# Layer 1's second product in 7 products of half blocks, its scale and bias on the result, ScalarE exponents, a new order

## The chip, the cores and the metric

The kernel runs on 1 core of a Trainium2 chip. The metric is the device time of that core in microseconds. Before the change the median of 3 runs is 805.74 us (804.72 to 806.02). One execution was profiled; its span, from the first instruction to the last, is 802.9 us.

## The reference

Attention runs within chunks of 64 positions, and its result goes through two layers. Inputs and results are float32, except that the weights of the layers lie in memory as 64-bit words, which the kernel itself turns into float32.

```python
# q, k, v: 4 batches x 8 heads x 576 positions x 64
scores = q_c @ k_c.T / sqrt(64)                # within each chunk of 64
attn = exp(scores - max); attn /= sum + 1e-9
x = attn @ v_c                                 # as 2304 tokens x 512
h = x @ w_in                                   # layer 1: 512 x 2048
x = (s * relu(h)**2 + b) @ w_out               #          2048 x 512; s, b: one number each
h = x @ w2_in                                  # layer 2
out = (max(h, 0) + log1p(exp(-abs(h)))) @ w2_out
```

## The kernel before

**Products.** A float32 product is made of three products of rounded halves: `split` cuts an operand into a high part (a CAST on ScalarE, L955) and the rest (a subtraction on VectorE, L964), and TensorE multiplies high by high, high by low and low by high. So a block of 128 rows, 128 sums and N = 384 tokens takes three matmuls of 384 columns.

**First products.** Both layers' first products use a scheme that makes a 2 x 2 product of half blocks with 7 products in place of 8. `quad(ph, i, j, ...)` makes, in layer `ph`, four blocks of hidden rows of pair `i` (of 8) for the group `j` (of 3) of 768 tokens (two halves of 384): products 1 to 7 (L1375, six matmuls each), copies between accumulators (L1397), four sums (`sub`, L942), and four hidden blocks (`hidden`, L1407: Relu in layer 1, Softplus in layer 2). The operands of the scheme are sums of halves of x (`even_forms`, `odd_forms`, `forms`) and of the weights (`weights1`).

**Second products.** In layer 1, each hidden block is stored to memory (`hid`, 192 KB). Then six blocks of results (3 groups x 2 halves, `block`) each run over 16 hidden rows x 4 output blocks x 3 matmuls (L1554). Hidden rows are loaded back four at a time (768 KB), squared on ScalarE (L1523), scaled by s with b added (L807 or L809) and split. The output weights are converted in advance by `weights2`, stored in `spill` (512 KB a pair) and loaded and split during the first block. In layer 2 the second product is `second_by_blocks`: 7 products x 3 groups x 8 steps x 6 matmuls (L1710). For it `quad` forms four sums more of the hidden blocks and stores seven arrays (`kept`, `summed`), `weights2` forms four sums more of the weights and stores seven arrays (`forms2`), and the results of the products are added into four result blocks.

**Weights.** `convert` turns 512 words of each of 128 rows into float32: the exponent is cut out (VectorE, L850), moved (ScalarE Relu, L867), the mantissa is put together (VectorE, L880 and L894), the sign is merged into the exponent (VectorE, L908), and mantissa and exponent are multiplied (VectorE, L922).

**Order.** All DMAs are issued from SyncE (`load`, L817). The order of every engine's instructions is made by `Work.order`: it steps through a modelled time, and among the operations that can start next takes the one with the smallest key. The keys are due times, from formulas in the code or from the table `PLAN`. The model gives each step a cost, and takes 300 KB per us for DMA (`BYTES`) and 2.0 us for a load (`LOAD`). Where an operation may run on either of two engines, the same search decides. `warmed` puts matmuls without a result (L1877) where TensorE would otherwise stand idle. Attention's steps (scores L1189, transposes L1290, values L1309) are woven with the first quads of layer 1.

## Time and profile before

| | |
|---|---|
| median of 3 runs | 805.74 us (804.72 to 806.02) |
| span of the profiled execution | 802.9 us |
| TensorE busy | 787.6 us, 98% |
| VectorE busy | 635.3 us, 79% |
| ScalarE busy | 514.2 us, 64% |
| DMA | 180.27 MB, mean 225 GB/s |

No other time of the profiled execution is recorded. The span falls into stages: the start to 8.0 us, attention with the first quads of layer 1 to 85.5, a transition to 95.2, the rest of layer 1's first product to 247.4, its second product to 447.7, layer 2's first product to 624.6, its second product to 799.4, and the last stores. The edges are where the kind of matmul changes. A row of windows gives the busy time of each engine in such a stretch; PE is TensorE's matmuls, PEld its weight loads, DVE VectorE, ACT ScalarE, POOL GpSimd, SP SyncE. Lines such as L942 are lines of the kernel before.

### The profile page before, as it was taken

Reading aid. Unit: us, or ns where it says so; the run is one execution under the profiler, and the core shown is the slowest. Engines: PE = TensorE matmul, PEld = TensorE weight load, DVE = VectorE, ACT = ScalarE, POOL = GpSimd, SP = SyncE. Lnnn points to the kernel's source line nnn. Section 1 sums busy time; section 2 is a strip of 40 time slices with the busy share of each in tenths; the row PEclk is TensorE's granted clock in tenths of the full one; section 3 lists DMA queues with packets and bytes.
Section 4 is the critical chain, followed back from the end, with each engine's and each line's share of the span. In section 5 each row is a group of like instructions: output and inputs, shape, how many; then the busy total and the mean of one; then the engine's idle time right before and its main releaser. Section 6 shows DMA issues by size and latency. Waiting matters only on the chain.

```text
span 802.9 us, 14597 instructions
## 1 busy us (share of the span) xinstructions
PE 787.6 (98%) x5148; PEld 772.8 (96%) x5148; DVE 635.3 (79%) x1167; ACT 514.2 (64%) x1127; POOL 138.9 (17%) x161
## 2 busy tenths in 40 slices
PE   7999999999999999999999999999999999999998
PEld 5788999999999999999999999999999999999998
DVE  6999898998858998889946786888876777777765
ACT  5877766666659867676765765655655566555543
POOL 3644311111110222123302220112010000000000
PEclk9999999999999999999999999999999999999999
DMA  7863477787679576766630056775788977678851
GB/s 275 277 192 111 162 251 234 265 274 259 221 237 370 207 243 196 269 212 211 225 113 1 31 194 226 243 252 200 256 287 288 388 284 241 231 236 289 275 191 59
DMA packets 78041, 180.27 MB, mean 225 GB/s; under 512 B 8720, under 2 KB 52752, under 8 KB 77072
## 3 DMA queue, kind: packets, MB, share of 16 engines
q1 hardware_dynamic: 77968, 179.34, 66.1%
q8 instruction: 40, 0.66, 0.3%
q14 instruction: 33, 0.27, 0.1%
HBM read 111.15 MB, written 68.16 MB: 223 GB/s over the span
## 4 chain that ended last, share of the span: by engine, by line
PE 92%; DVE 5%; issue 1%; DMA 1%; ACT 1%; POOL 1%; SPq 0%; DVEq 0%; POOLq 0%; ACTq 0%
PE at L1375 19%; PE S L1375 13%; PE S L1554 9%; PE at L1554 9%; PE A L1375 9%; PE S L1710 8%; PE at L1710 8%; PE A L1554 6%; PE A L1710 5%; DVE operands L964 1%; PE at L1309 1%; PE at L1189 1%; DMA last<-spill 1%; PE at L1290 1%; DVE mx L1203 1%
## 5 line engine op out<-in xcount | busy, mean ns | idle before, releaser
L942 POOL TENSOR_TENSOR mem<-mem 128x256 f32<-128x256 f32 x120 | 105.0, 885 | 382.3 <-DVE mem L922 296.5
L964 DVE TENSOR_TENSOR operands<-mem,operands 128x384 fp32r<-128x384 f32 (+4 forms) x186 | 128.4, 709 | 38.6 <-ACT operands L955 37.2
L955 ACT CAST operands<-mem 128x384 fp32r<-128x384 f32 (+4 forms) x186 | 112.0, 622 | 58.6 <-PE at L1710 36.2
L964 DVE TENSOR_TENSOR operands<-last,operands 128x384 fp32r<-128x384 f32 (+2 forms) x184 | 108.3, 609 | 48.8 <-ACT operands L955 38.7
L955 ACT CAST operands<-last 128x384 fp32r<-128x384 f32 (+2 forms) x184 | 93.3, 528 | 58.1 <-PE at L1710 18.4
L1375 PE MATMUL at<-operands 128*128 128x384 f32 x624 | 121.0, 336 | 0.0
L1375 PEld LDWEIGHTS at<-operands 128*128 128x128 f32 x624 | 109.4, 188 | 0.5 <-DVE mem L942 0.2
L1710 PE MATMUL at<-operands 128*128 128x384 f32 x384 | 87.1, 334 | 0.0
L1710 PE MATMUL S<-operands 128*128 128x384 f32 x384 | 87.1, 334 | 0.0
L1554 PE MATMUL S<-operands 128*128 128x384 f32 x432 | 85.1, 335 | 1.0 <-ACT operands L955 0.8
L1554 PE MATMUL at<-operands 128*128 128x384 f32 x432 | 83.2, 334 | 0.0
L1375 PE MATMUL S<-operands 128*128 128x384 f32 x420 | 82.9, 336 | 0.0
L1554 PEld LDWEIGHTS S<-operands 128*128 128x128 f32 x432 | 75.7, 188 | 1.5 <-ACT operands L955 1.1
L1554 PEld LDWEIGHTS at<-operands 128*128 128x128 f32 x432 | 75.7, 188 | 0.0
L942 DVE TENSOR_TENSOR mem<-mem 128x384 f32<-128x384 f32 (+1 forms) x108 | 60.4, 566 | 19.2 <-ACT mem L1407 14.6
L1375 PEld LDWEIGHTS S<-operands 128*128 128x128 f32 x420 | 73.8, 188 | 0.1
L1710 PEld LDWEIGHTS at<-operands 128*128 128x128 f32 x384 | 68.4, 188 | 0.0
L1710 PEld LDWEIGHTS S<-operands 128*128 128x128 f32 x384 | 68.4, 188 | 0.0
L1375 PE MATMUL at<-last,operands 128*128 128x384 f32 x336 | 66.0, 336 | 0.6 <-ACT S L1397 0.6
L1407 ACT ACTIVATE mem<-S 128x384 f32<-128x384 f32 x104 | 50.4, 490 | 24.4 <-PE S L1375 21.8
L1375 PE MATMUL A<-operands 128*128 128x384 f32 x300 | 60.6, 340 | 1.3 <-DVE A L942 1.3
L1397 ACT COPY S<-at 128x384 f32<-128x384 f32 x80 | 37.3, 467 | 37.4 <-PE at L1375 33.0
(87 smaller groups left out, 1237.0 us busy)
## 6 DMA issues: line engine op xcount, KB each, us to landing
mem<-in_w_dram SPq DMA_DIRECT2D x64, 512.0 KB, 4.5
summed<-mem SPq DMA_DIRECT2D x168, 192.0 KB, 2.2
mem<-summed SPq DMA_DIRECT2D x30, 768.0 KB, 5.5
hid<-mem SPq DMA_DIRECT2D x96, 192.0 KB, 3.2
last<-hid SPq DMA_DIRECT2D x24, 768.0 KB, 5.4
last<-in_qk_dram SPq DMA_DIRECT2D x36, 256.0 KB, 3.7
last<-summed SPq DMA_DIRECT2D x12, 768.0 KB, 5.2
mem<-forms SPq DMA_DIRECT2D x7, 1024.0 KB, 7.0
```

The source lines that it names most:

```text
L942: lambda e: on(e).tensor_tensor(out=out(), in0=x(), in1=y(), op=op or ALU.subtract),
L955: lambda e: nc.scalar.copy(out=hi().bitcast(F32R), in_=x()),
L964: lambda e: nc.vector.tensor_tensor(out=lo().bitcast(F32R), in0=x(), in1=hi(), op=ALU.subtract),
L1189: nc.tensor.matmul(out_[c * D : (c + 1) * D, pr], of("q")[:, pr * P + c * D : pr * P + (c + 1) * D], kb[:, :, pr, c, :], start=True, stop= ...
L1203: lambda e: nc.vector.tensor_reduce(out=mx[:, :, 0], in_=heads(at(sc)), op=ALU.max, axis=AX.X),
L1290: nc.tensor.transpose(at(pt)[:, c], of("e")[:, c], ident)
L1309: nc.tensor.matmul(at(px)[y, x], of("v")[y, x], of("aT")[y, x], start=True, stop=True)
L1375: nc.tensor.matmul(acc(dst)().rearrange("p (u c) -> p u c", u=GROUP), l[a], r[c], start=start and kk == 0 and x == 0, stop=kk == 1 and x == 2,
L1397: lambda e: nc.scalar.copy(out=acc(place)(), in_=acc(ba)()),
L1407: lambda e: nc.scalar.activation(out=at(go), in_=acc(place)(), func=AF.Softplus if ph else AF.Relu),
L1554: nc.tensor.matmul(at(accs[d])[:, :N], l[a], r[c], start=m == 0 and z == 0, stop=m == NM - 1 and z == 2,)
L1710: nc.tensor.matmul(at(accs[d])[:, :N], l[a], r[c], start=i == 0 and y == 0, stop=i == NF - 1 and y == 2,)
```

## The change

Layer 1's second product becomes `second_by_blocks(0, ...)`, as in layer 2; `block`, `hid` and `spill` go. Therefore in layer 1, too, `quad` squares the four hidden blocks (on ScalarE or VectorE), forms the four further sums and stores seven arrays, and `weights2` forms and stores seven arrays of the weights. A pair of hidden blocks is now split in one step of 768 columns, in both layers.

The scale s and the bias b are applied to the result: b times the column sums of the weights. Those sums come from products with two more columns of ones (`edge`), so that in three of the 21 steps (products 1, 2 and 5 of the first group) the matmuls have 386 columns. The results are multiplied by s, with the bias added, on VectorE or ScalarE.

`convert` has two forms. In the one used for 44 of the 64 conversions (`leaky`) ScalarE makes the exponent from the words' upper 16 bits (or VectorE by a shift), and two Prelu steps on ScalarE give the exponent with the sign, so that the merge on VectorE goes. The other form is the former one.

Sums (`sub`) and the subtraction of a split may run on GpSimd or VectorE, as the table says. `PLAN` now holds a rank for each operation, with a letter where there is a choice of engine, and `Work.order` takes each engine's operations by rank. The last two pairs of layer 1's first product are now run group by group. Four of layer 2's eight pairs of `weights2`, and two of its `weights1`, come during layer 1's second product. 

```diff
-    BYTES = 300e3
+    STORE, LOAD, FIRST = 1.6, 2.3, 3.0
+    BYTES = 330e3
...
-    "quad0 4 1": (160.36, 93.12, 157.98, 159.24, 161.1, 163.91, 162.43, 143.76, 108.75, 166.77, 167.6, 162.14, 163.4, 164.01, 166.3, 167.57, 168.17, 170.46, 172.15, 173.14,),
...
+    "quad0 4 1": "908 913 923 932 938 947 965 970 983 979 982 930 942 956 951 961 966 1010 1028 1036V 1006 986 969 1040 1047G 1054 1058 1060 1075 1057 1078",
...
+        def exponent(e):
+            if e == "ACT":
+                halves = at(f).bitcast(I16).rearrange("p (a b) -> p a b", b=4)
+                nc.scalar.activation(
+                    out=a().bitcast(I32), in_=halves[:, :, 3], func=AF.Copy, scale=1 / 16, bias=-15 / 32
+                )
...
+        if leaky:
+            o1 = add(
+                {"ACT": act(DM), "DVE": dve(DM, True)}, key, exponent, [ld], [f, am], after=turn.get(("am", part), ())
+            )
...
+            o2 = add({"ACT": act(DM)}, key, leak(1.0, -896.0, 2.0**-40, af, ai), [o1], [am])
+            o5 = add({"ACT": act(DM)}, key, leak(2.0**23, 1792 * 2.0**-17, 2.0**40, ai, af), [o2], [am])
...
-    def sub(key, out, x, y, n, deps, uses=(), op=None, e="DVE", port=True, **kw):
+    def sub(key, out, x, y, n, deps, uses=(), op=None, port=True, **kw):
         return add(
-            {e: pool(n) if e == "POOL" else dve(n, port=port)},
+            {"DVE": dve(n)} | ({"POOL": pool(n)} if n < 512 else {}) if port else {"DVE": dve(n, port=False)},
...
-            out_ = lambda: hid[ph][2 * j + half][:, 2 * i + row]
-            st = load(key + 0.1, out_, lambda: at(go), P * N * 4, [o], [go])
-            hid_in.setdefault((ph, j, half), []).append(st)
-            quads_done[ph].append(st)
+
+            def square(e):
+                if e == "ACT":
+                    nc.scalar.activation(out=at(go), in_=at(go), func=AF.Square)
+                else:
+                    nc.vector.tensor_tensor(out=at(go), in0=at(go), in1=at(go), op=ALU.mult)
+
+            return go, add({"ACT": act(N), "DVE": dve(N)}, key, square, [o], [go])
...
-        if not ph:
-            return
...
+            edged = not ph and j == groups[0] and n in (1, 2, 5)
+            width = N + 2 if edged else N
...
+                if i % 2 == 0:
+                    pair = divided((a + i % 4 * N, 2 * N), key, ld)
+                hi, lo = [(x, width) for x, y in pair[i % 2]]
...
+                        add(
+                            {"ACT": act(N, False, 2), "DVE": dve(N, True, 2)},
+                            t,
+                            lambda e, dst=dst, x=to // 2 * 2 + d: scaled(e, mem(*dst, v), x),
+                            [biased[(5 if to > 1 else 2), d], *scalars],
+                            w=[dst],
+                        )
...
-    for z, x in enumerate(BLOCKS):
-        block(0, x // 2, x % 2, end + z * dt, z == 0)
+    second_by_blocks(0, end)
```

How the order moves, at three places. In these rows a name before the arrow is written, a name behind it read; `A_`, `S_` and `at_` are TensorE's accumulators, `operands` holds split operands, `mem` and `last` are working memory, and x6 counts equal instructions in a row. Lines of the new kernel are other lines than those of the one before.

TensorE at the end of attention, before: the last values step is L1309, products of layer 1 are L1375.

```order
L1375 MATMUL A_66<-operands 128x384 x6
L1375 MATMUL S_67<-operands 128x384 x6
L1375 MATMUL A_66<-operands 128x384 x6
L1290 MATMUL at_70<-ident,last_117 128x128 x4
L1309 MATMUL at_72<-last_117 64x64 x16
L1309 MATMUL at_70<-last_117 64x64 x16
L1375 MATMUL A_66<-operands 128x384 x6
L1375 MATMUL S_68<-operands 128x384 x6
L1375 MATMUL S_69<-operands 128x384 x6
L1290 MATMUL at_71<-ident,last_117 128x128 x4
L1375 MATMUL A_65<-operands 128x384 x6
L1309 MATMUL at_72<-last_117 64x64 x16
```

The same place after; values are L1421 there, transposes L1402, products L1487.

```order
L1421 MATMUL at_71<-last_134 64x64 x16
L1421 MATMUL at_72<-last_134 64x64 x16
L1402 MATMUL at_70<-ident,last_134 128x128 x4
L1421 MATMUL at_72<-last_134 64x64 x16
L1402 MATMUL at_70<-ident,last_134 128x128 x4
L1402 MATMUL at_71<-ident,last_134 128x128 x4
L1421 MATMUL at_70<-last_134 64x64 x16
L1421 MATMUL at_71<-last_134 64x64 x16
L1487 MATMUL A_66<-operands 128x384 x12
L1487 MATMUL A_65<-operands 128x384 x6
L1487 MATMUL A_66<-operands 128x384 x6
L1487 MATMUL S_67<-operands 128x384 x6
```

Before, single products stand between the last attention steps; after, the last eight steps of attention stand together and the products follow them. Ahead of the last values step stood 15 products, and now 7.

TensorE where layer 1's second product begins, before (first product L1375, second L1554).

```order
L1375 MATMUL A_66<-operands 128x384 x6
L1375 MATMUL at_72<-operands 128x384 x6
L1375 MATMUL S_68<-operands 128x384 x6
L1375 MATMUL A_65<-operands 128x384 x6
L1554 MATMUL S_67<-operands 128x384 x6
L1554 MATMUL at_71<-operands 128x384 x6
```

The same place after (first product L1487, second L1755).

```order
L1487 MATMUL S_69<-operands 128x384 x6
L1487 MATMUL at_72<-operands 128x384 x6
L1755 MATMUL S_69<-operands 128x386 x3
L1755 MATMUL at_70<-operands 128x386 x3
L1487 MATMUL S_67<-operands 128x384 x6
L1755 MATMUL S_69<-operands 128x386 x3
L1755 MATMUL at_70<-operands 128x386 x3
L1487 MATMUL A_65<-operands 128x384 x6
L1487 MATMUL S_68<-operands 128x384 x6
L1755 MATMUL S_68<-operands 128x384 x3
L1755 MATMUL at_71<-operands 128x384 x3
```

Before, the second product begins after the last product of the first; after, four half steps of it, with 386 columns, stand ahead of the last three products. On SyncE's queue at that place, before (`hid` and `spill` are the stores, `last` is where the second product's operands are loaded):

```order
L817 DMA hid_5_90<-mem 128x384
L817 DMA last_2578<-spill_91 128x512 x3
L817 DMA hid_5_90<-mem 128x384
L817 DMA last_2578<-hid_4_89 128x1536 x2
L817 DMA hid_0_85<-mem 128x384
L817 DMA last_2578<-spill_91 128x512 x6
L817 DMA hid_2_87<-mem 128x384
L817 DMA last_2578<-hid_4_89 128x1536
```

And after (`summed` and `forms` are stores where they are written, loads where they are read):

```order
L905 DMA last_2842<-summed_1_2_87 128x1536
L905 DMA summed_3_1_92<-mem 128x384
L905 DMA summed_7_2_105<-mem 128x384
L905 DMA last_2842<-forms_0_127 128x1024
L905 DMA summed_5_1_98<-mem 128x384
L905 DMA summed_4_2_96<-mem 128x384
L905 DMA summed_5_2_99<-mem 128x384
L905 DMA summed_2_1_89<-mem 128x384
L905 DMA last_2842<-summed_1_0_85 128x1536
L905 DMA summed_2_2_90<-mem 128x384
L905 DMA summed_6_2_102<-mem 128x384
L905 DMA last_2842<-summed_1_2_87 128x1536
```

Before, 9 stores of hidden blocks stand behind the first load of the second product; after, 27 stores of sums do, and the loads of sums and of weight forms are woven with them.

VectorE in the middle of layer 1's first product, before (L850 exponent, L880 and L894 mantissa, L908 sign, L922 product, L942 sum).

```order
L850 TENSOR_SCALAR mem<-mem 128x512
L880 TENSOR_SCALAR mem<-mem 128x512
L894 SCALAR_TENSOR_TENSOR mem<-mem 128x512
L908 SCALAR_TENSOR_TENSOR mem<-mem 128x512
L922 SCALAR_TENSOR_TENSOR mem<-mem 128x512
L942 TENSOR_TENSOR A_65<-at_70,mem 128x384
L850 TENSOR_SCALAR mem<-mem 128x512
L880 TENSOR_SCALAR mem<-mem 128x512
L894 SCALAR_TENSOR_TENSOR mem<-mem 128x512
L908 SCALAR_TENSOR_TENSOR mem<-mem 128x512
```

The same stage after (L947 exponent, L1016 and L1030 mantissa, L1044 product, L1064 sum, L1534 square).

```order
L1064 TENSOR_TENSOR mem<-at_72,mem 128x384
L1534 TENSOR_TENSOR mem<-mem 128x384
L1016 TENSOR_SCALAR mem<-mem 128x512
L1064 TENSOR_TENSOR mem<-mem 128x384
L1064 TENSOR_TENSOR mem<-mem 128x256
L1064 TENSOR_TENSOR mem<-mem 128x384
L1030 SCALAR_TENSOR_TENSOR mem<-mem 128x512
L1064 TENSOR_TENSOR mem<-at_71,mem 128x384
L1044 SCALAR_TENSOR_TENSOR mem<-mem 128x512
L1064 TENSOR_TENSOR mem<-mem 128x384
L947 TENSOR_SCALAR mem<-mem 128x512
L1064 TENSOR_TENSOR mem<-mem 128x256 x2
```

Before, a conversion has five rows on VectorE with few sums between them; after, it has three or four, and sums of 384 and 256 elements and a square stand between them.

## Rows read from the trace of the kernel before

**Rows 1.** Busy time of each engine, share of the span, and instructions (the page):
```profile
PE 787.6 (98%) x5148; PEld 772.8 (96%) x5148; DVE 635.3 (79%) x1167; ACT 514.2 (64%) x1127; POOL 138.9 (17%) x161
```

**Rows 2.** Windows: length, busy (instructions) by engine, granted clock, DMA share, GB/s:
```profile
8.00:85.50 77.50, 71.92 (x1048) 60.74 (x1044) 70.32 (x150) 61.08 (x214) 35.38 (x38) 1.00 0.65 215
...
95.20:247.40 152.20, 150.88 (x864) 149.48 (x862) 128.48 (x221) 96.78 (x193) 24.18 (x30) 1.00 0.76 252
...
247.40:447.70 200.30, 200.09 (x1152) 199.83 (x1153) 161.66 (x296) 143.60 (x294) 42.99 (x46) 1.00 0.59 193
...
447.70:624.60 176.90, 175.59 (x1011) 175.08 (x1010) 138.43 (x245) 106.02 (x218) 29.54 (x32) 1.00 0.66 229
...
624.60:799.40 174.80, 174.80 (x1009) 174.56 (x1008) 124.40 (x237) 96.91 (x192) 0.00 (x0) 1.00 0.72 245
```

**Rows 3.** Groups by line, TensorE, 0 to 85 us: busy, mean ns | idle before:
```profile
L1877 PE MATMUL S<-nought 128*128 128x512 f32 x31 | 10.3, 439 | 0.0
```

**Rows 4.** Groups kept apart by form, VectorE and ScalarE:
```profile
L908 DVE SCALAR_TENSOR_TENSOR mem<-mem 128x512 uint32<-128x512 uint32 x34 | 23.5, 692 | 1.2 <-ACT mem L867 1.2
...
L850 DVE TENSOR_SCALAR mem<-mem 128x512 uint32<-128x512 uint32 x34 | 15.7, 463 | 11.9 <-DMA mem<-in_w_dram 11.6
...
L964 DVE TENSOR_TENSOR operands<-mem,operands 128x1024 fp32r<-128x1024 f32 x15 | 18.8, 1256 | 0.0
...
L964 DVE TENSOR_TENSOR operands<-mem,operands 128x768 fp32r<-128x768 f32 x9 | 10.2, 1133 | 2.4 <-ACT operands L955 2.4
...
L802 DVE COPY last<-at 128x512 f32<-128x512 f32 x7 | 4.7, 674 | 0.5 <-ACT mem L1407 0.3 <-PE at L1290 0.2
...
L942 DVE TENSOR_TENSOR mem<-mem 128x256 f32<-128x256 f32 x6 | 2.5, 413 | 3.2 <-ACT mem L800 3.2
...
L867 ACT ACTIVATE mem<-mem 128x512 int32<-128x512 int32 x34 | 21.6, 635 | 17.9 <-DVE mem L850 17.9
...
L1523 ACT ACTIVATE last<-last 128x384 f32<-128x384 f32 x96 | 45.2, 515 | 5.9 <-DMA last<-hid 5.8
```

**Rows 5.** Timeline of VectorE, then ScalarE: start us, us, engine, line, operation:
```profile
540.69 0.69 DVE L908 SCALAR_TENSOR_TENSOR mem<-mem 128x512 uint32<-128x512 uint32 x1
541.29 0.55 DVE L942 TENSOR_TENSOR mem<-mem 128x384 f32<-128x384 f32 x1
541.76 0.69 DVE L922 SCALAR_TENSOR_TENSOR mem<-mem 128x512 f32<-128x512 f32 x1
...
455.95 0.49 ACT L1407 ACTIVATE mem<-S 128x384 f32<-128x384 f32 x1
456.34 0.61 ACT L955 CAST operands<-last 128x512 fp32r<-128x512 f32 x1
456.85 0.49 ACT L1407 ACTIVATE mem<-S 128x384 f32<-128x384 f32 x1
```

**Rows 6.** DMA, 95.2 to 247.4: total; issues with KB, us to landing:
```profile
DMA packets 18379, 38.38 MB, mean 252 GB/s; under 512 B 2288, under 2 KB 12427, under 8 KB 18367
...
hid<-mem SPq DMA_DIRECT2D x81, 192.0 KB, 3.3
...
spill<-mem SPq DMA_DIRECT2D x8, 512.0 KB, 5.3
```

**Rows 7.** Windows, as in rows 2, of three stretches with much DMA:
```profile
600.00:650.00 50.00, 50.00 (x290) 50.00 (x289) 33.75 (x64) 29.49 (x62) 0.00 (x0) 1.00 0.92 329
...
235.00:240.00 5.00, 5.00 (x30) 5.00 (x30) 2.29 (x4) 2.40 (x5) 0.00 (x0) 1.00 0.96 303
...
165.00:170.00 5.00, 5.00 (x30) 5.00 (x29) 4.45 (x9) 2.39 (x6) 1.84 (x3) 1.00 0.79 209
```

**Rows 8.** Windows as in rows 2: start of layer 2, and inside layer 1:
```profile
455.00:460.00 5.00, 3.69 (x21) 3.37 (x21) 3.56 (x7) 4.31 (x9) 1.43 (x2) 1.00 0.24 88
...
275.00:300.00 25.00, 25.00 (x146) 25.00 (x145) 23.85 (x44) 19.17 (x39) 4.51 (x5) 1.00 0.61 201
```

691 lines of the change are left out of this document (328 added, 363 removed), and 906 rows, old and new, of the table PLAN.

## Prediction

> **What bounds the kernel now.** I read the busy table first, then the stages, then the stages' other engines. The busy table gives TensorE 98% of the span [rows 1]. A busy share alone could hide slow matmuls, so the windows by stage come next; the granted clock is 1.00 in each, the level of 2.4 GHz [rows 2]. Layer 1's second product fills 247.40 to 447.70 with 1152 matmuls and layer 2's fills 624.60 to 799.40 with 1008 (the row counts one that straddles its edge); PE is busy for 200.09 of 200.30 us and all of 174.80. Both run at 0.174 us per matmul of 384 columns, back to back. The same holds in the two first products after 85.5 us. Only the attention stretch, 8.0 to 85.5, is otherwise: PE shows 71.92 busy, but 31 of its matmuls are fillers without a result [rows 3], and DVE is busy for 70.32 of 77.5 us. There DVE sets the pace; after it PE does. So a matmul taken from a back-to-back stage is worth its 0.174 us, provided that what feeds and empties PE still keeps up. That proviso is the question here, since the change buys its matmuls with DVE, ACT and DMA work in layer 1's first product.
>
> **The change part by part.** Durations are of one execution with a span of 802.9 us. The page records no other time of it; against the median of 805.74 shown, 2.84 us lie outside the span, and I add them back at the end.
>
> *Fewer matmuls.* 6 blocks of 16 x 12 (1152) become 7 products x 3 groups x 8 x 6 (1008). The kernel already holds both forms, so the price is a difference of two stages: 200.30 - 174.80 = 25.5 us [rows 2]. Three of the 21 steps run 386 columns instead of 384: 144 matmuls x 2/384 x 0.174 = 0.13 us. Term: **-25.4**.
>
> *Attention stretch.* The exponents go to ACT and the order is new. Up to the last reciprocal of the attention the new DVE order has four sign merges fewer (0.692 each), three exponent shifts (0.463), one split of 1024 (1.256) and one of 768 (1.133), four copies of 512 (0.674) and one difference of 384 (0.55), and two more sums of 256 (0.41): 2.77 + 1.39 + 1.26 + 1.13 + 2.70 + 0.55 - 0.83 = 9.0 us less on the engine that sets the pace [rows 4, 5]. But the last attention matmul now follows 7 products where it followed 15, by the order, and those 8 x 6 x 0.174 = 8.3 us are run afterwards: 0.7 us gained. The order drops 9 of the 31 fillers at 10.3/31 = 0.33 us each [rows 3], which says up to 3.0 us gained. Against it, ACT was busy for 61.08 of 77.5 us and takes at least 8 more conversions (0.635) and the four copies: about 69 us in a stretch of 68.5, so it could cost as much as it gives, up to +3. I take **-1.0**, next to the DVE sum.
>
> *Layer 1's first product, DVE and ACT.* Stretch 95.2 to 247.4, DVE busy 128.48 of 152.2, ACT 96.78 [rows 2]. Each of the 24 quads gains four sums and four squares of 384. By the new order 76 of the 96 sums and 19 of the squares stand on DVE, 77 squares on ACT, the other 20 sums on POOL. DVE also gains about 25 sums of 256 for the weights' forms; it loses some 30 sign merges and 18 exponent shifts, and ACT gains 48 conversions. By durations that is 128.5 + 95 x 0.55 + 25 x 0.41 - 30 x 0.69 - 18 x 0.46 = 162 us for DVE, and 96.8 + 77 x 0.515 + 48 x 0.635 = 167 us for ACT [rows 4]: both over 152. Durations overstate it, though. When the next instruction waits ready, it starts before the last one's row ends: a sum of 384 shows 0.55 but the next starts 0.47 later, an operation of 512 shows 0.69 and 0.60, on ACT 0.61 and 0.51, 0.49 and 0.38 [rows 5]. Packed, DVE's 221 rows cost 0.08 each less, 111 us, and the change adds 95 x 0.47 + 25 x 0.34 - 30 x 0.60 - 18 x 0.38 = 28 (0.34 and 0.38 are estimates, the 0.41 and 0.46 less 0.08): 139 of 152. ACT: 97 - 193 x 0.10 + 77 x 0.41 + 48 x 0.53 = 135. So 91% and 89%, with PE still last. The ends are 0 and +15 (167 - 152). I take **0**: the rows of a full engine are the nearest. What hides the squares and sums is PE; if the cover goes, PE waits for free accumulators.
>
> The Trainium skill, "VectorE: DVE Perf Modes", section "The DRAIN you can't avoid", says that the next Vector operation does not start until the pipe has emptied. Held to the letter, it would leave no overlap and put DVE at 162 us; that case is the second rival. The trace disagrees here by the 0.47 beside 0.55.
>
> *Layer 1's first product, DMA.* The stretch moved 38.38 MB at a share of 0.76 [rows 2, 6]. The stage now stores 168 sums of 192 KB where it stored 96, and in the new SP order 27 of them stand behind the first load of the second product, where 9 did: 54 more here, 10.6 MB. The forms of the weights are 896 KB a pair where the spill was 512: 8 x 0.39 = 3.1 MB. So 52.1 MB. At a full share the stretch's own row gives 252/0.76 = 332 GB/s, or 157 us: +4.7. The row 600 to 650, with the same stores beside loads, gives 329/0.92 = 358, or 145.5 us: nothing. The poorest busy row gives 303/0.96 = 316, or 165 us: +12.7 [rows 7]. I take **+3.0**, between the first two. If it binds, the stores hold the result buffers, ACT cannot empty the accumulators, and PE waits.
>
> The Trainium skill, "DMA: Bandwidth & Descriptors", section "Specifications", gives about 358 GB/s of HBM per core. By it the term would be 0 (52.1 MB in 145.5 us, an estimate), and the sum 3 us less; the row of 600 to 650 agrees, the stretch itself lies below.
>
> *Both ends of the second product.* PE lost 1.3 us in the stretch that ends where layer 1's products meet (150.88 of 152.2) [rows 2] and 1.31 where layer 2 begins (455 to 460) [rows 8]. In the new order two steps of the second product stand between layer 1's last products, and the forms for layer 2 wait for the very last sums: after the two scaled sums of group 0, DVE has 9 us of sums and splits to do before the third product, beside 8 steps of the last group (8.3 us) and two first products (2.1). It fits by 1.2 us. Ends: -2 and +3; I take **0**. Within the stage DVE has 84 splits of 768, 28 of 512, 58 sums and some conversions, about 170 us of 175 by durations and 150 packed, so PE leads. Layer 2's own stages keep their matmuls; its first product takes eight conversions more where DVE was busy for 138.43 of 176.9 [rows 2], at 0.
>
> *Sum.* 802.9 - 25.4 - 1.0 + 0 + 3.0 + 0 = 779.5 us of span, + 2.84 = **782 us**.
>
> **The rivals.** *DMA is full in layer 1.* For it: 342 GB/s wanted, above 332; the 24 first steps of the second product want six loads of 768 KB, two of the forms and the late stores in 25 us. Against: rows at 0.92 beside a PE without a gap. At 316 GB/s the term is 12.7 instead of 3.0: 792 us.
>
> *DVE and ACT become the bound in layer 1's first product*, either because packing does not hold or because they wait for each other: three conversions in a row on ACT feed a DVE operation, and a sum waits for four squares. For it: 91% and 89% at once, which no stage had. Against: from 275 to 300 DVE was busy for 23.85 of 25 us and PE for all 25 [rows 8]. With +10 (162 - 152): 792 us.
>
> *Everything fits and the start gains.* -3 at the start instead of -1, no DMA term, -2 at the ends: 782.3 - 2 - 3 - 2 = 775 us. For it: the fillers dropped, and the HBM rate of the row 600 to 650. Against: ACT, full at the start.
>
> *Slower than before.* One mechanism: the stores crowd the DMA queues so that small packets set the rate. The row 165 to 170 moved 209 GB/s at a share of 0.79, so 264 when full [rows 7]: 52.1 MB take 197 us, 45 more than the stretch has, and the result is 824 us. It decides from 292 GB/s down (52.1 / (152.2 + 26.4)), where the whole gain is gone. Against it: three of the four rates above are over 300.
>
> *The saving does not arise*, since PE waits at each step for the splits of 768: against it, layer 2's second product, which does the same with splits of 384, shows no gap in 174.8 us. It counts within the second rival.
>
> **How the numbers follow.** Forecast 782: 0.62, with an own range of 777 to 787. DMA full: 0.16. DVE and ACT: 0.11. Everything fits: 0.08. Slower: 0.03. The range that holds the time 8 times in 10 runs from 775 to 793: the forecast's bounds, the better case, and the two at 792; outside lie the slower case and the outer halves of the rest. A measurement of this kernel tells about 0.2% from no change. Faster by more than that: 0.96; within it: 0.01; slower: 0.03.
>
> **What would show it.** Layer 1's second product should take 174 to 176 us with 1008 matmuls and no gap over 1 us inside. In the 150 us before it DVE and ACT should be near 90% busy and DMA at a share of 0.9 or more with PE busy throughout. The last attention matmul should end near 77 us. A DMA share at 1.0 with ACT waiting for DMA on the results' buffers, and PE short of 24.5 in any 25 us there, shows the first rival; DVE at 25 of 25 with PE waiting for ACT or DVE shows the second. The forecast is wrong if the second product takes more than 180 us, or if the first one ends later than it did (247).

## The result and the profile after

The changed kernel takes 814.54 us (median of 4 runs, 813.73 to 816.11) against 805.24 us of the kernel before: a ratio of 1.012, with a 95% interval of 1.0106 to 1.0135. It is slower by 1.2%; the forecast was 782 us, in a range of 775 to 793. The profiled execution has a span of 813.0 us.

The busy table of the page after, which answers to [rows 1]:

```profile
PE 775.7 (95%) x4995; PEld 750.5 (92%) x4995; DVE 671.7 (83%) x1181; ACT 533.3 (66%) x1068; POOL 126.1 (16%) x132
```

TensorE lost the 144 matmuls of the forecast and 9 fillers, but its busy time fell by 12 us only, and it is idle for 37 us of the span where it was for 15. The windows show where. They have the columns of [rows 2]; the edges are the changed kernel's own: the last attention matmul, two cuts in the first product, then the ends of the stages (276.0 is where the second product would begin if its 1008 matmuls ran at 0.1735 us each, without a gap, to its end at 451.0).

```profile
8.00:78.80 70.80, 62.51 (x983) 51.83 (x983) 66.03 (x139) 64.50 (x221) 34.95 (x36) 0.98 0.72 235
78.80:100.00 21.20, 17.23 (x94) 16.14 (x93) 18.64 (x41) 17.69 (x38) 1.83 (x2) 0.98 0.35 120
100.00:246.00 146.00, 140.40 (x775) 135.37 (x774) 134.13 (x253) 123.02 (x256) 28.40 (x28) 0.99 0.93 302
246.00:276.00 30.00, 22.29 (x117) 19.88 (x116) 21.08 (x42) 19.98 (x42) 6.38 (x7) 1.00 0.93 300
276.00:451.00 175.00, 174.86 (x995) 174.18 (x995) 156.26 (x245) 117.82 (x178) 18.32 (x17) 0.99 0.80 282
451.00:634.00 183.00, 179.29 (x1014) 176.00 (x1014) 157.95 (x302) 108.57 (x225) 32.90 (x32) 1.00 0.78 260
634.00:809.00 175.00, 174.40 (x1005) 173.79 (x1003) 114.20 (x157) 80.40 (x111) 0.00 (x0) 1.00 0.69 249
```

The account, stage by stage. The second product counts 175.0 us where it took 200.3: 25.3 saved. The 175.0 follow from where the edge is put; what the trace shows of them is that TensorE is busy for 174.86 of the last 175.00 us before 451. The product's true first matmul stands at 266.9, ahead of the first product's last one, which ends at 272.6, and from 266.9 on it takes 184 us. Ahead of the edge 28.6 us were lost, since it lies at 276.0 in place of 247.4. Layer 2, to the end of the span, takes 362.0 us where it took 355.2: 6.8 lost. The sum, -25.3 + 28.6 + 6.8, is the 10.1 us between the spans.

In the 28.6, attention has a part of 1.6: its last matmul ends 6.7 us earlier (78.8 for 85.5), but 8 products fewer stand ahead of it, and these are worth 8.3. The other 27.0 are layer 1's first product. From 78.8 to 276.0 it has 161 products left, 966 matmuls at 0.1735, which is 167.6 us in 197.2: 29.6 lost. Before, 153 products (159.3 us) ran in the 161.9 us from 85.5 to 247.4: 2.6 lost.

What TensorE waited for from 78.8 to 276 (engine, tile and line, what it waited for: us in total, times, longest):

```profile
PE S L1755 <- ACT mem L1520: 4.7, 2, 2.8
PE A L1487 <- DVE A L1064: 3.9, 3, 1.7
PE S L1487 <- DVE S L1064: 2.3, 1, 2.3
PE at L1487 <- ACT S L1509: 1.9, 4, 0.6
PE A L1487 <- ACT S L1509: 1.6, 2, 1.1
```

And what ScalarE and VectorE waited for behind that, of the same stretch:

```profile
ACT mem L1520 <- DVE mem L1064: 7.8, 6, 3.1
ACT mem L1520 <- DMA summed<-mem: 7.2, 6, 4.7
...
DVE mem L1064 <- DMA summed<-mem: 5.8, 3, 2.4
```

No single releaser stands out. TensorE waits for accumulators that ScalarE (L1520, the hidden blocks; L1509, the copies) or VectorE (L1064) has not emptied or filled; ScalarE waits for sums of VectorE and for stores that still hold its buffers; VectorE waits for stores. The DMA of 100 to 276 us, beside [rows 6]:

```profile
DMA packets 32632, 53.09 MB, mean 302 GB/s; under 512 B 3168, under 2 KB 28512, under 8 KB 32617
...
summed<-mem SPq DMA_DIRECT2D x145, 192.0 KB, 4.0
...
forms<-mem SPq DMA_DIRECT2D x8, 512.0 KB, 5.0
```

A part of the loss is TensorE's clock. Three waits were followed by about 3.5 us at 0.50 (start, us, engine, line, idle before):

```profile
10.12 1.81 PE L1300 MATMUL A<-last 128*64 128x128 f32 x16 [2.46 <-DMA last<-in_qk_dram]
11.86 3.45 PE L1981 MATMUL S<-nought 128*128 128x512 f32 x10
...
98.25 1.61 PE L1487 MATMUL S<-operands 128*128 128x384 f32 x6 [2.33 <-DVE S L1064]
...
275.43 0.91 PE L1755 MATMUL S<-operands 128*128 128x384 f32 x3 [2.81 <-ACT mem L1520]
...
276.80 1.17 PE L1755 MATMUL S<-operands 128*128 128x386 f32 x3
...
280.37 0.68 PE L1755 MATMUL S<-operands 128*128 128x386 f32 x3
```

Three matmuls take 1.17 us at 276.80 and 0.68 at 280.37. In windows, around the first of the dips and in two of them:

```profile
10.50:13.50 3.00, 3.00 (x18) 2.39 (x15) 2.54 (x9) 3.00 (x18) 0.97 (x1) 0.50 0.69 262
...
277.00:280.00 3.00, 3.00 (x11) 3.00 (x10) 2.30 (x3) 2.67 (x6) 0.00 (x0) 0.50 0.95 335
```

0.50 is the level of 1.2 GHz. The kernel before had 1.00 in all these stages [rows 2]. Each dip costs some 1.7 us, half of its length (an estimate: the same matmuls at 1.00 would take half).

### The profile page after: what moved, and what is told of

Same layout as the page of the kernel before. It is cut to its first block, busy times and chain, and to the rows that moved or that the text cites. A ratio compares the mean times of both kernels' runs of the same rounds, so it can differ in the third digit from the quotient of the medians.

```text
span 813.0 us, 14302 instructions
## 1 busy us (share of the span) xinstructions
PE 775.7 (95%) x4995; PEld 750.5 (92%) x4995; DVE 671.7 (83%) x1181; ACT 533.3 (66%) x1068; POOL 126.1 (16%) x132
## 4 chain that ended last, share of the span: by engine, by line
PE 63%; DVE 8%; DMA 6%; ACT 5%; issue 2%; POOL 0%; SPq 0%; DVEq 0%; ACTq 0%; POOLq 0%
PE S L1755 15%; PE at L1755 15%; PE at L1487 13%; PE A L1755 10%; PE S L1487 6%; DMA summed<-mem 5%; PE A L1487 4%; DVE mem L1064 2%; DVE operands L1086 2%; ACT mem L1520 1%; ACT operands L1077 1%; DMA last<-summed 1%; DVE last L1086 1%; ACT mem L956 1%; ACT mem L1532 1%
## 5 line engine op out<-in xcount | busy, mean ns | idle before, releaser
L1755 PE MATMUL S<-operands 128*128 128x384 f32 (+1 forms) x768 | 176.4, 337 | 4.8 <-ACT mem L1520 4.7
L1755 PE MATMUL at<-operands 128*128 128x384 f32 (+1 forms) x768 | 175.3, 335 | 0.0
L1086 DVE TENSOR_TENSOR operands<-mem,operands 128x768 fp32r<-128x768 f32 (+3 forms) x150 | 132.8, 908 | 41.3 <-ACT operands L1077 40.8
L1077 ACT CAST operands<-mem 128x768 fp32r<-128x768 f32 (+3 forms) x150 | 115.3, 792 | 72.4 <-PE at L1755 39.0
L1064 POOL TENSOR_TENSOR mem<-mem 128x256 f32<-128x256 f32 (+1 forms) x95 | 92.2, 978 | 432.3 <-DVE mem L1044 229.9
L1077 ACT CAST operands<-last 128x768 fp32r<-128x768 f32 (+2 forms) x136 | 103.8, 781 | 81.1 <-PE at L1755 39.2
L1064 DVE TENSOR_TENSOR mem<-mem 128x384 f32<-128x384 f32 (+1 forms) x261 | 131.6, 521 | 25.1 <-DMA summed<-mem 9.5
L1755 PEld LDWEIGHTS S<-operands 128*128 128x128 f32 x768 | 137.3, 189 | 6.4 <-ACT mem L1520 5.3
L1086 DVE TENSOR_TENSOR operands<-last,operands 128x768 fp32r<-128x768 f32 (+2 forms) x132 | 118.5, 914 | 25.0 <-ACT operands L1077 24.2
L1755 PEld LDWEIGHTS at<-operands 128*128 128x128 f32 x768 | 137.7, 189 | 0.0
L1487 PE MATMUL at<-operands 128*128 128x384 f32 x624 | 120.7, 337 | 4.5 <-ACT S L1509 3.5
L1487 PEld LDWEIGHTS at<-operands 128*128 128x128 f32 x624 | 108.5, 188 | 8.3 <-ACT S L1509 4.9
L1755 PE MATMUL A<-operands 128*128 128x384 f32 (+1 forms) x480 | 89.3, 335 | 0.0
L1487 PE MATMUL S<-operands 128*128 128x384 f32 x420 | 85.0, 338 | 2.3 <-DVE S L1064 2.3
L1755 PEld LDWEIGHTS A<-operands 128*128 128x128 f32 x480 | 83.9, 188 | 0.1
L1487 PEld LDWEIGHTS S<-operands 128*128 128x128 f32 x420 | 74.3, 189 | 3.0 <-DVE S L1064 2.7
L1520 ACT ACTIVATE mem<-S 128x384 f32<-128x384 f32 x104 | 50.7, 490 | 36.7 <-DMA summed<-mem 13.8
L1487 PE MATMUL at<-last,operands 128*128 128x384 f32 x336 | 68.6, 341 | 2.9 <-DVE mem L889 1.3
L1487 PE MATMUL A<-operands 128*128 128x384 f32 x300 | 62.5, 346 | 7.2 <-DVE A L1064 4.5
L1487 PEld LDWEIGHTS at<-last,operands 128*128 128x128 f32 x336 | 59.1, 188 | 5.3 <-ACT S L1509 1.8
L1487 PEld LDWEIGHTS A<-operands 128*128 128x128 f32 x300 | 52.7, 191 | 11.3 <-DVE A L1064 5.7
```

The costliest lines, as they stand in the source:

```text
L1064: lambda e: on(e).tensor_tensor(out=out(), in0=x(), in1=y(), op=op or ALU.subtract),
L1077: lambda e: nc.scalar.copy(out=hi().bitcast(F32R), in_=x()),
L1086: lambda e: on(e).tensor_tensor(out=lo().bitcast(F32R), in0=x(), in1=hi(), op=ALU.subtract),
L1487: nc.tensor.matmul(acc(dst)().rearrange("p (u c) -> p u c", u=GROUP), l[a], r[c], start=start and kk == 0 and x == 0, stop=kk == 1 and x == 2,
L1520: lambda e: nc.scalar.activation(out=at(go), in_=acc(place)(), func=AF.Softplus if ph else AF.Relu),
L1755: nc.tensor.matmul(at(accs[d])[:, :width], l[a], r[c], start=i == 0 and y == 0, stop=i == NF - 1 and y == 2,)
```

## The experiments

Three theories were set against each other. A: DMA traffic sets the length of layer 1's first product. B: VectorE's and ScalarE's work does. C: the order of the instructions does, since each queue issues strictly one after the other, so that a late step holds what is queued behind it. Ratios are to the kernel before, measured beside each run (804.5 to 805.0 us). Lines of a trace are of one execution; where that one lies far from the median, it is said.

**Half of each sum stored.** The stores take 64 of the 128 partitions, and each load becomes two that fetch these 64, for either half of its tile (only the stores' edit is shown).

```diff
-            st = load(key, lambda: summed[ph, n, j][:, i], lambda: at(go), P * N * 4, [o], [go])
+            rows = P if ph else P // 2
+            st = load(key, lambda: summed[ph, n, j][:rows, i], lambda: at(go)[:rows], P * N * 4, [o], [go])
```

> The changed kernel, but layer 1's sums are stored from 64 of the 128 partitions only, and the loads of the second product fetch these 64 twice: 168 stores of 96 KB in place of 192 KB, all else and the order unchanged (half of the sums is left out of the result). Theory A (the DMA traffic of layer 1's first product sets its length: stores hold the buffers, ScalarE and VectorE wait for free buffers, TensorE for accumulators): some 15 MB less before 276 us at about 300 GB/s; the second product begins near 250 us instead of 276, the clock dips before it go, and the time is 785 to 798 us. Theory B (VectorE at 92% and ScalarE at 84% busy between 100 and 246 us, waiting for each other, set the length): no change beyond 3 us, 811 to 817. Theory C (the order is a bad one by itself, whatever the transfers take): no change beyond 3 us either.

Measured: 839.62 us, outside of every theory. The first product got shorter by some 6 us (its successor begins at 261.1 for 266.9), but the second product took 215 us from its first matmul to its last, where it took 184: ScalarE waited 52 us for its loads. DMA of 280 to 470 us in this run:

```profile
DMA packets 13549, 45.65 MB, mean 240 GB/s; under 512 B 1856, under 2 KB 5851, under 8 KB 13537
...
last<-summed SPq DMA_DIRECT2D x73, 384.0 KB, 7.7
```

and of 280 to 450 us in the changed kernel:

```profile
DMA packets 14078, 48.15 MB, mean 283 GB/s; under 512 B 1343, under 2 KB 6129, under 8 KB 14065
...
last<-summed SPq DMA_DIRECT2D x37, 768.0 KB, 5.8
```

Where one load of 768 KB stood, two of 384 KB, to 64 partitions each, stand one behind the other, so the 7.7 us are not the price of one alone. The Trainium skill, "SBUF — State Buffer", section "Door 1: The DMA port swizzle (why `[64,N]` ≈ `[32,N]`)", says that DMA bandwidth goes by how many of the 16 ports the partitions reach; by its table the first 64 reach 8. The trace agrees in direction: the two halves land later than the whole (7.7 us beside 5.8), and the rate of all transfers fell from 283 to 240 GB/s. The experiment failed, as its edit added a cost of its own; it was made again in another way (below).

**No squares.** The emission of the 96 squares is left out.

```diff
             def square(e):
...
+                pass
```

> The changed kernel without the 96 squares of layer 1's hidden blocks (left out of the result), all else and the order unchanged: 77 operations of 0.41 to 0.52 us less on ScalarE and 19 of 0.47 to 0.55 on VectorE, the same bytes. Theory A (DMA traffic): 810 to 816 us, no change beyond 4 us, since every store still takes its turn. Theory B (VectorE and ScalarE): some 10 us less on VectorE and 32 on ScalarE; the first product of layer 1 ends 8 to 15 us earlier and the time is 799 to 807. Theory C (the order): in between, as a chain through a square gets 0.5 us shorter.

Measured: 807.43 us (ratio to the kernel before 1.003, 1.0012 to 1.0048). 7 us of the loss come back: 0.4 us above B's range, under A's, and in between, as C has it. The ten executions spread from 804.27 to 810.43. DMA stays at 0.93, 306 GB/s.

**Exponents and signs back on VectorE.**

```diff
-        if leaky:
+        if False:
```

> The changed kernel with all 64 weight conversions in the former form (exponent by a shift on VectorE, one Relu on ScalarE, sign merge on VectorE) at the same places of the order: in 44 conversions one operation of 0.63 us goes over from ScalarE to VectorE, and the exponents that ScalarE made too. Theory A (DMA traffic): 812 to 820 us, since VectorE is late only where a store isn't. Theory B (VectorE at 92%): VectorE gets some 25 us more before 276 us and passes 100%; the time is 828 to 840. Theory C: 815 to 825.

Measured: 842.6 us, as B says and 2.6 over it. From 100 to 246 us (columns of [rows 2]):

```profile
100.00:246.00 146.00, 131.11 (x690) 124.02 (x691) 136.61 (x257) 93.22 (x196) 25.30 (x24) 0.96 0.82 266
```

VectorE is the fullest engine here by far (ScalarE has 64%, DMA 0.82), and it shows 136.6 of 146 us, 94%. A full VectorE of this kernel reads about 94 to 96, not 100: the highest share on record is the 95.6% of order e with half of the sums (below).

**The kernel before with more stores.** 72 hidden blocks are stored a second time, to arrays that nobody reads.

```diff
+            if (row, half) != (0, 0):
+                once = st.emit
+
+                def twice(e):
+                    once(e)
+                    nc.sync.dma_start(out=extra[2 * row + half - 1, j][:, i], in_=at(go))
+
+                st.emit = twice
```

> The kernel before the change, with 72 of layer 1's 96 hidden blocks stored a second time to an array that nobody reads: 14.2 MB more, some 12 of them between 95 and 247 us, which makes about 50 MB in the 152 us of that stage; no engine computes more. Theory A (DMA traffic): the stage gets 8 to 25 us longer and the time is 813 to 830 us. Theory B (VectorE and ScalarE, which have no more to do): 804 to 808, no change beyond 2 us. Theory C (the order of the changed kernel): no change either, since this is the other order.

Measured: 819.09 us (1.0186, 1.0165 to 1.0206): 14 us slower with no more work for any engine.

```profile
100.00:246.00 146.00, 138.57 (x761) 134.41 (x760) 115.66 (x202) 82.60 (x166) 21.85 (x26) 0.98 0.89 301
```

Against the same window of the unchanged kernel before:

```profile
100.00:246.00 146.00, 145.42 (x834) 144.35 (x833) 122.64 (x211) 91.75 (x181) 22.15 (x28) 1.00 0.77 254
```

834 matmuls became 761 with VectorE at 79% and ScalarE at 57% (this execution took 822.0 us, the slowest of four). So the stores alone, at 300 GB/s, make TensorE wait, as A says; B and C, which expected no change here, don't hold alone, and by the run before A doesn't either. The way that the prediction gave for DMA, stores that hold the result buffers, is the smaller part of it: ScalarE waited 4.2 us for the second stores and 1.0 for the first. VectorE waited far longer for the weights to be loaded, from 89 to 266 us here (first two lines) and from 85.5 to 247.4 in the kernel before (last line):

```profile
DVE mem L851 <- DMA mem<-in_w_dram: 21.0, 12, 3.8
ACT mem L1408 <- DMA extra<-mem: 4.2, 4, 2.2
...
DVE mem L850 <- DMA mem<-in_w_dram: 7.2, 8, 1.8
```

Whether the loads came late because of the bytes, or because 72 more transfers stand ahead of them on the one queue, was not told apart.

**Half of the sums stored,** for every second pair, with transfers of the same shape (the loads, whose edit is not shown, fetch the stored half twice).

```diff
+            slot = i if ph else i // 2
+            st = load(key, lambda: summed[ph, n, j][:, slot], lambda: at(go), P * N * 4, [o], [go])
+            if not ph and i % 2:
+                st.emit = lambda e: None
```

> The changed kernel, but layer 1's sums are stored for every second pair of hidden blocks only (84 stores of 192 KB in place of 168), and the loads of the second product fetch those twice; the shape of each transfer, the loads, the order and all engines' work are unchanged (half of the sums is left out of the result). In the earlier run with half the partitions the loads became slow, so that it told little of the stores. Theory A (DMA traffic sets the length of layer 1's first product): 16.5 MB less, of which some 14 MB between 100 and 276 us where 302 GB/s moved; the second product begins at 246 to 255 us and the time is 786 to 798 us. Theory B (VectorE and ScalarE): 808 to 815. Both bounds near each other, so that removing one leaves the other: 796 to 808.

Measured: 808.34 us (1.0041, 1.0028 to 1.0054), 6 us back: less than A, within B's and just over what two near bounds would give. DMA went from 0.93 to 0.72 in the window, and the matmuls only from 775 to 777.

**Half of the sums and no squares,** the two edits above together.

> The run before, and the 96 squares left out as well (both left out of the result), order unchanged. Theory A alone: the same as with half the sums, within 3 us. Theory B alone: the same as without squares alone (807 us), within 3 us. Both bounds near each other: less than either, 784 to 796 us, and the first product of layer 1 without a gap over 1 us after 100 us, its second product beginning near 247 us.

Measured: 803.86 us (0.9992, 0.9974 to 1.001). 11 us back of the 33 between measurement and forecast. All three expectations were missed, the second by 0.1 us.

**No squares and no further sums.**

```diff
+        if not ph:
+            for o in (o1, o2, o3, o4):
+                o.emit = lambda e: None
```

> The changed kernel without the 96 squares and without the 96 sums of hidden blocks in layer 1 (both left out of the result; the buffers are stored all the same, so the bytes and the order are unchanged): 76 operations of 384 elements less on VectorE and 20 on GpSimd beyond the run without squares (807 us). Theory A (DMA traffic alone): 803 to 808 us, as without squares. Theory B (VectorE and ScalarE): VectorE has some 45 us less in layer 1's first product, which then is 15 to 20 us shorter than in the changed kernel: 792 to 799 us. Theory C (the order lets a late store or a late sum hold what is queued behind it, whatever the cause): 798 to 805, as a shorter chain helps but the stores still come late.

Measured: 804.33 us (0.9987, 0.9973 to 1.0), though VectorE fell to 99.2 of 146 us: A and C, not B.

**All three less:** half of the sums stored, no squares, no further sums (the three edits above).

> The changed kernel with half of layer 1's sums stored, and without the squares and the further sums (all left out of the result), order unchanged: between 100 and 246 us DMA is at a share near 0.7 as with half the sums, VectorE near 68% and ScalarE near 72% busy as without sums and squares. If the loss comes from the resources being nearly full together (VectorE 92%, ScalarE 84%, DMA 0.93 in the changed kernel), so that relieving one leaves the others, the loss goes now: 825 matmuls or more between 100 and 246 us (775 in the changed kernel, 834 in the one before), the second product begins before 250 us, and the time is 782 to 792 us. If the order itself leaves TensorE idle whatever the others do: 797 to 803 us, as with two of the three relieved, and some 800 matmuls.

Measured: 799.61 us (0.9948, 0.9923 to 0.9974).

```profile
100.00:246.00 146.00, 143.91 (x807) 140.46 (x808) 99.21 (x187) 104.96 (x208) 9.67 (x12) 1.00 0.74 240
```

With VectorE at 68%, ScalarE at 72% and DMA at 0.74, TensorE still runs 807 matmuls, where 146 us have room for 841 and the kernel before ran 834. That is 6 us in this window, and the time stays 18 us over the forecast. So nearly full resources are not the whole cause. What holds the rest is the order, as the expectation has it, or a chain of steps that no run took away.

Where the time came back can be read in the traces. From the last attention matmul to the end of layer 1's second product, 1974 matmuls are left; against 0.1735 us for each, this stretch loses 30 us in the changed kernel, 25 with half of the sums stored, 24 without squares, 20 without sums and squares, 19 with half of the sums and no squares, and 16 with all three less. The kernel before loses 3 there. So 14 of the 27 us come back, and 13 stay. About 4 of these can be named: where the second product takes up again after its first four half steps, TensorE waits 2.8 to 3.0 us for ScalarE (L1520) in each of these six traces, whatever was relieved, and mostly a dip of the clock follows.

**New orders a and b.** The same operations and bytes; only the table differs, and the planner's DMA rate with which it was searched.

```diff
-    BYTES = 330e3
+    BYTES = 303e3
```

> The changed kernel with another table: the same operations and bytes, but the order of each engine (and the choice between VectorE and GpSimd, or ScalarE, where there is one) searched again with 303 KB per us for the DMA, which is what the trace of the changed kernel shows in layer 1's first product, in place of 330. Theory C (the order was made for faster transfers and holds work behind late ones): 790 to 803 us. Theories A and B (too many bytes, or too much work for VectorE and ScalarE, whatever the order): 809 to 816, no gain beyond 5 us.

> As the run before, from another start of the search, with an end that the search's own costs put within 0.4 us of it. Theory C: 790 to 803 us, and within 4 us of the run before. Theories A and B: 809 to 816.

Measured: 813.71 (1.0107, 1.0092 to 1.0122) and 817.93 us (1.0159, 1.0142 to 1.0177); b is over every range, and 4.2 us from a. C in this form failed: a lower DMA rate alone made no better order. A possible reason, not tested by itself, can be read in the trace of the changed kernel. ScalarE's exponent (L943) is followed by the next step after 0.56 to 0.59 us:

```profile
132.15 0.66 ACT L943 ACTIVATE mem<-mem 128x512 int32<-128x512 int16 x1
132.71 0.48 ACT L1520 ACTIVATE mem<-S 128x384 f32<-128x384 f32 x1
...
142.03 0.68 ACT L943 ACTIVATE mem<-mem 128x512 int32<-128x512 int16 x1
142.62 0.51 ACT L1532 ACTIVATE mem<-mem 128x384 f32<-128x384 f32 x1
```

The planner's formula (0.09 + 512 x 0.00083) gives it 0.515.

**New orders c and d.** As before, with the costs taken from the trace, and searched for transfers that land early or late.

```diff
-    STORE, LOAD, FIRST = 1.6, 2.3, 3.0
-    BYTES = 330e3
+    STORE, LOAD, FIRST = 1.8, 2.15, 3.2
+    BYTES = 322e3
...
-                {"ACT": act(DM), "DVE": dve(DM, True)}, key, exponent
+                {"ACT": act(DM) + 0.056, "DVE": dve(DM, True)}, key, exponent
```

> The changed kernel with a third table: the same operations and bytes; the order searched again, and this time with the costs that the trace of the changed kernel shows for each kind of step (ScalarE's exponent 0.57 us where the table's costs had 0.515, its split of 768 columns 0.74 for 0.727, GpSimd's sum of 384 elements 1.24 for 0.957, DMA at 322 KB per us with 1.8 us for a store), with an idle TensorE of over 2.2 us counted as slow afterwards, and for the mean of an undisturbed course and two in which transfers land up to 2 us early or late. Theory C (the order has no room for steps that take a few per cent longer and transfers that land late, so that each delay is handed on through the in-order queues): the second product of layer 1 begins at 250 to 262 us, no stretch at clock 0.50 of several us before it, and the time is 794 to 804 us, under the kernel before. Theories A and B (too many bytes, or too much work for VectorE and ScalarE, in any order): 809 to 817, as in the two new orders before, which kept the old costs.

> As the run before, from another start and for the mean of one undisturbed course and one with transfers that land early or late. Theory C: 794 to 804 us, within 4 us of the run before. Theories A and B: 809 to 817.

Measured: 807.64 (1.0042, 1.0019 to 1.0066) and 809.63 us (1.0066). 5 to 7 us back, half of what C said; c meets neither range, and d lies in that of A and B, at its lower end. Several costs were changed at once, so it isn't shown which of them made the order better.

**New orders e and f,** the search taken further, with more disturbed courses; again only the table and the planner's costs differ (350 KB per us, 1.83 us for a store and others).

> The changed kernel with a fourth table: the search of the order taken further from the third one, for the mean of one undisturbed course and three in which transfers land up to 2.5 us late or 1 us early, with the landing times that five of the traces show (350 KB per us, 0.3 us more for each load of weights, 1.83 us for a store). Same operations and bytes. Theory C (the order, in queues that issue strictly one after the other, is what costs the time): 793 to 801 us, under the kernel before (804.7), with the second product of layer 1 beginning at 252 to 262 us. Theory of nearly full resources (VectorE and ScalarE at 85 to 93% and DMA at 0.93, whatever the order): no better than the third table, 805 to 811.

> As the run before, from another course of the search. Theory C: 794 to 803 us, within 4 us of it. Theory of nearly full resources: 805 to 811.

Measured: 803.72 (0.9993, 0.9979 to 1.0007) and 807.72 us. With nothing left out, order e brings 11 us back and is level with the kernel before; it does not beat it. It lies between the two ranges; f lies in that of nearly full resources. The window of order e, in an execution of 807.46 us, its slowest of twelve:

```profile
100.00:246.00 146.00, 141.50 (x786) 137.82 (x785) 137.31 (x277) 131.25 (x275) 2.69 (x3) 0.99 0.96 314
```

VectorE is at 94%, the share that it showed where it was the fullest, ScalarE at 90%, and DMA at 0.96. GpSimd, busy for 28.40 us in the changed kernel, has 2.69: the table also moved sums from it to VectorE. So what the 11 us show is the worth of the table, order and choice of engine together. The second product now begins when the first has ended, and the wait of 2.8 us at its beginning is gone; the longest there is 1.3 (this execution has another, of 2.54 us, at 292.7).

**Order e, relieved.** The two edits of above, in order e.

> The fourth order (804 us) with half of layer 1's sums stored (left out of the result), all else unchanged. In that order DMA is at a share of 0.96 to 0.98 from 100 to 270 us, VectorE at 94% and ScalarE at 90% between 100 and 246. If DMA is what is left in it: 16.5 MB less give 10 us or more, 786 to 795 us, with the second product of layer 1 beginning before 254 us. If VectorE and ScalarE are: 799 to 804 us.

> The fourth order without the 96 squares (left out of the result), all else unchanged. If ScalarE and VectorE are what is left in it: 77 or so operations less on ScalarE and 20 on VectorE give 7 us or more, 790 to 797 us. If DMA is: 800 to 804 us.

Measured: 798.95 (0.9921, 0.9898 to 0.9943) and 800.53 us (0.9949, 0.9929 to 0.9969). 5 and 3 us: each resource holds a part, neither the whole. The first is at the edge of the range for VectorE and ScalarE, the second in that for DMA. With half of the sums, VectorE goes higher than anywhere else:

```profile
100.00:246.00 146.00, 143.44 (x803) 140.91 (x802) 139.54 (x281) 131.95 (x277) 3.65 (x4) 0.99 0.76 243
```

**More fillers early.** Five more matmuls without a result ahead of the second scores.

```diff
+                more = 5 if op is second else 0
-                for x in range(int((op.start - t - spare) / self.IDLE) if t else 2):
+                for x in range(more + int((op.start - t - spare) / self.IDLE) if t else 2):
```

> The changed kernel with 5 more matmuls without a result ahead of the second product of the scores, where TensorE stood idle for 2.46 us (waiting for a load of q and k) and then ran from 10.4 to 13.6 us at a granted clock of 0.50. If the idle time is what took the clock down, the clock stays at 1.00 there, 10 us of fillers and scores run at 0.24 to 0.44 us in place of twice that, and the attention stretch ends 0.5 to 1.7 us earlier, as some of those slow matmuls are fillers too: 812.5 to 814.3 us. If the clock falls for another cause, or if VectorE sets the end of that stretch whatever TensorE does: 814 to 815.5.

Measured: 815.62 us, no gain. The clock did stay up:

```profile
9.83 1.09 PE L1302 MATMUL A<-last 128*64 128x128 f32 x16 [1.18 <-DMA last<-in_qk_dram]
10.85 2.59 PE L1983 MATMUL S<-nought 128*128 128x512 f32 x10
```

Ten fillers take 2.59 us where they took 3.45, and the last attention matmul ends at 78.0 for 78.8. The 0.8 us were lost again by 276 us, where this run has a dip more (265 to 268). So at this place the idle time did take the clock down, and five more fillers in it cost nothing.

**No late conversions in layer 2.** Of layer 2, the conversions of part 1 of the weights that VectorE makes (not leaky) are left out.

```diff
+        if ph and part and not leaky:
+            for o in (o1, o2, o3, o4, o5, o6):
+                o.emit = lambda e: None
```

> The changed kernel without the eight weight conversions that it puts into layer 2's first product (their arithmetic is left out of the result, their loads and everything after stay): some 20 us of VectorE less there. If VectorE is what makes layer 2's first product 183 us long where it was 177, the stage comes back to 176 to 179 us and the time is 808 to 811 us. If DMA (260 GB/s there) or the order makes it longer: 813 to 816.

Measured: 814.6 us (1.0134, 1.0096 to 1.0171), no change, with VectorE's busy time from 470 to 600 us down from 119.7 to 101.3. VectorE does not make layer 2's first product longer.

## Why the prediction was wrong

**Fewer matmuls: right.** -25.4 forecast. Once it has taken up again at 275.4, the second product runs to its end without a gap and, after the dip, at the price per matmul of layer 2's. Its beginning is another matter (below): from 266.9 it takes 184 us, over the 180 that the prediction gave as a sign of being wrong, and the first product ends at 272.6, not by 247.

**Attention: wrong by 2.6.** -1.0 forecast, +1.6 measured. VectorE's busy time in the stretch fell by 4.3 us (70.32 to 66.03) where 9.0 less were counted up to the last reciprocal. VectorE is busy for 93% of the 70.8 us and ScalarE for 91%; which of them holds the stretch isn't shown. TensorE's own longest wait there is for a load of q and k (2.46 us), and the dip of the clock behind it costs some 1.7. The 3 us of the fillers were no gain, but the run with five more of them shows only that these cost nothing in that idle time.

**Layer 1's first product: here the prediction failed.** The step that failed is "139 of 152 ... So 91% and 89%, with PE still last", with "I take 0" behind it, and the +3.0 for DMA on its own. The measured loss is 27.0 us.

First, VectorE's sum was too small. It took the overlap of rows (0.08 us each, 111 for 128.5) off a window's busy time, which counts overlapped rows once already. The rows of VectorE from 95.2 to 247.4 show it. The five largest of their sixteen groups:

```profile
L894 DVE SCALAR_TENSOR_TENSOR mem<-mem 128x512 f32<-128x512 uint32 x30 | 21.0, 701 | 0.5
L922 DVE SCALAR_TENSOR_TENSOR mem<-mem 128x512 f32<-128x512 f32 x30 | 20.7, 690 | 0.8
L908 DVE SCALAR_TENSOR_TENSOR mem<-mem 128x512 uint32<-128x512 uint32 x30 | 20.5, 684 | 1.2 <-ACT mem L867 1.2
L880 DVE TENSOR_SCALAR mem<-mem 128x512 uint32<-128x512 uint32 x30 | 14.9, 497 | 0.0
L850 DVE TENSOR_SCALAR mem<-mem 128x512 uint32<-128x512 uint32 x30 | 14.1, 470 | 7.6 <-DMA mem<-in_w_dram 7.2
```

All sixteen add up to 139.8 us, where the window has 128.48 for the same 221 rows. Packed they are 139.8 - 17.7 = 122, and with the 28 that the change adds 150 of 152 us: 99%, not 91. ScalarE, whose rows add up to 104.1 us, comes to 142 of 152 in the same way, not to 135.

Second, the 92% that VectorE shows from 100 to 246 us does not confirm the 91. That the two are alike is luck: only 775 matmuls ran there, where the forecast's pace is 841. For each matmul that ran, VectorE was busy for 0.173 us (134.13 / 775), DMA for 0.175 (0.93 x 146 / 775) and ScalarE for 0.159, beside TensorE's own 0.1735. At the forecast's pace, and if the work is spread evenly, that is 100, 101 and 91%: an estimate, but it leaves VectorE and DMA no room. For DMA, 302 GB/s at 0.93 are 325 when full; at that rate the forecast's 52.1 MB take 160 us, 8 more than the stretch had, not 3.0.

Third, each resource was taken by itself, and the stage's length was set by the longest. Relieving one gives 6 or 7 us, two 10 or 11, all three 15, and another table of the same operations 11. These are parts of one loss, and no run gave it back whole.

**The rivals.** DMA full and VectorE and ScalarE as the bound were both priced as if the other weren't there (792 us each), and both hold a part. "The saving does not arise" did not happen: after 275.4 the second product never waits. The slower case had 0.03, by a rate of 264 GB/s when full, and the rate was 325. Its time of 824 us is nearer than the forecast by luck; its mechanism did not happen.

**Both ends of the second product: wrong.** Taken at 0, since the work ahead of the third step "fits by 1.2 us". In the 30 us to 276, TensorE ran 117 matmuls (20.3 us), with waits of 1.84 and 2.81 us for ScalarE, and 3.5 us at half clock behind the second. This is a part of the 27.0, not one more term. In the kernel before, the like place lost 1.3.

**Layer 2: wrong by 6.8, taken at 0.** It isn't VectorE's conversions, by the run without them. It isn't the bytes alone either: from the end of layer 1's second product to the end of the span, the traces with the changed kernel's order and an unaltered layer 2 take 360.2 to 362.4 us, those of orders a to f, with the same bytes, 356.8 to 360.7 (least in d), and the kernel before 355.0. So up to 5 of the 6.8 us go with the table (one trace each); what in the table does it stays open.

**What stays open.** With all three relieved, layer 1 still loses 13 us more than in the kernel before, and the cause of some 9 of them isn't shown. Order e, at 804 us, is still 22 us over the forecast. For each matmul it has VectorE, DMA and ScalarE busy for 0.175, 0.178 and 0.167 us, so the first two are full again, and relieving one gives 3 to 5 us. Whether a yet better order exists was not settled.

## What to carry to other kernels

Before taking work from an engine at nothing, ask what share that engine shows when it is known to be full, and measure the room from there, not from 100%. A window's busy time has overlapping rows in it once; don't take the overlap off again. And when a stage got longer, compare an engine's busy time for each unit of the stage's work, not its share of the longer time. Where a change fills two or three resources of one stage at once, price them together, as a chain through in-order queues: the stage's length is not the largest of their busy times. And an order searched with a cost model carries that model's errors: replay it with the costs of the trace, some steps late, before believing in its last per cents (here tables made so gave 5 to 11 us back, where a mended DMA rate alone gave none).

## What the runs showed of the hardware

TensorE's granted clock fell to 0.50 for some 3.5 us after idle times of 2.33, 2.46 and 2.81 us, and in the changed kernel not after one of 1.84. The length of one idle time does not settle it: with half of the sums and no squares it stayed at 1.00 after 2.95 us (first two lines: three matmuls in 0.68 us behind it), and with more fillers it fell after 1.84 (last line: three in 1.17).

```profile
263.89 0.80 PE L1755 MATMUL S<-operands 128*128 128x384 f32 x3 [2.95 <-ACT mem L1520]
264.53 0.68 PE L1755 MATMUL at<-operands 128*128 128x384 f32 x3
...
264.74 1.17 PE L1757 MATMUL S<-operands 128*128 128x386 f32 x3 [1.84 <-ACT mem L1522]
```

Half of a tile's bytes, over 64 of the 128 partitions, took far more than half of its time: stores of 96 KB landed after a median of 3.0 us, in a stretch that moved 228 GB/s, and stores of 192 KB after 4.0, at 302. An operation of ScalarE that reads every fourth 16-bit half takes 0.68 us for 512 elements, where the Relu on 32-bit words took 0.635 [rows 4].
